# A two-layer memory-attention kernel with a planned instruction order: new plan figures, the V weights loaded in eight pieces, and a new order of tasks

## The chip, the cores and the metric

The kernel runs on one NeuronCore of a Trainium2 chip. A core has five engines that run side by side, each with its own in-order stream of instructions: TensorE (matmuls; PE in the profile, its weight loads PEld), VectorE (DVE), ScalarE (ACT), GpSimd (POOL) and SyncE (SP), which here only issues DMAs. Engines meet through semaphores. Matmul results go to PSUM, of which the kernel uses eight banks (`bank`), and are copied from there to SBUF by ACT or DVE. The metric is the device time of one execution in microseconds (us); less is better.

## The reference

The program is two identical layers over a sequence of 2048 rows of width 512; a layer is attention with a small recurrent memory, then a gated feed-forward block (FFN), each behind a layer norm and with a residual:

```python
for s in range(n_seg):                       # 64 segments of 32 rows
    xs = x[:, s*seg_len:(s+1)*seg_len, :]
    h = jnp.concatenate([mem, xs], axis=1)   # 8 memory rows + 32 rows
    q, k, v = h @ Wq, h @ Wk, h @ Wv         # 32 heads of 128
    p = _softmax(masked(q @ k.T * scale)); o = (p @ v) @ Wo
    mem = o[:, :M, :]                        # feeds the next segment
    outs.append(o[:, M:, :])
...
x = x + _A_ref(_layernorm(x), mem0, ...)     # attention
x = x + _B_ref(_layernorm(x), ...)           # (sigmoid(x@w_gate) * (x@w_up)) @ w_down
x = x + _A_ref(_layernorm(x), mem0, ...)     # second layer, same weights
x = x + _B_ref(_layernorm(x), ...)
```

(The einsums are abridged to products.) Inputs and output are bf16. Because `mem` goes from one segment to the next, a layer has 64 steps in a row that can't overlap.

## The kernel before

**Tiling.** Work is cut into 70 steps. In step t, `emit_step` treats segment t of layer 1 and segment t-6 of layer 2 together, so that a matmul has 80 moving columns (two times 8 memory and 32 sequence rows) while both layers run, and 40 in the first six steps and the last six, where one layer runs alone. A step makes q and k per head (L834, weights `wq_sb`, `wk_sb`), copies them (`qku`), scores (L848), softmax on DVE and ACT (L862 to L879), transposes the probabilities (L891), multiplies with V (L914, V rows in `vsb`) and projects with `wo_sb` (L932). The next step's q and k need the memory rows that come out of this L932. After every fourth step a block of 128 rows goes through `ffn` (transposes L1002, gate and up L1034, down L1058), whose weights POOL loads anew for every block.

**V.** V of the sequence rows doesn't depend on the memory. `v_pass` (L682) multiplies 128 normed rows with eight column groups of `wv_sb`, four matmuls of 512 columns for each, and writes the results through small staging tiles (slices of the FFN weights' tiles `wd`, `wg`, `wu` in the start-up) to a DRAM scratch `scr`. In the start-up eight such passes are made for layer 1 (`trace`, `v_group`). V of the memory rows is made within each step (`strips`, L759, 32 matmuls), staged in `sst` and sent to `vsb`. Steps read their V rows back from `scr` by DMA (L803).

**Start-up.** x blocks and all weights are loaded by SP (`load_x` L721, `pre1` L736, `load_weights` L583). A block is normed by `layernorm_T`: statistics on DVE (L638 to L640), a power on POOL (L641), scaling on DVE (L642), four transposes on PE (L651), then copies to `xvf` (the left operand of a V pass) or to `hT` (the input of a step). POOL first clears `qku`, `ptsb`, `pb` and `hT` tiles (`clear`).

**What sets the order.** Every piece of work is a task with a list of engines, a duration, a latency and keys for its dependencies (`Planner.add`). `plan` takes the tasks' priorities from the compressed table `SEQUENCE`. `forward` then plays the tasks through: each engine, when free, takes the ready task of highest priority whose buffers are free. It models DMA transfers as one bus: a transfer starts at least LEAD after its issue, takes bytes/BUS, and is taken as landed TAIL after its end, or at the issue's end plus `lat`, whichever is later. The instructions are then written out in the order of the planned starts, so a plan fixes the order on every engine but not the times. Where the plan leaves PE idle for over 0.25 us, `warm` (L410) puts matmuls on a zero tile `hot` (L1150) ahead of the next task, to keep its clock up. PE works in order, so they take their time whether the wait is there or not. For the large POOL transfers a manual dependency on a PE instruction (`pace`) keeps them from starting early. SP has at most eight transfers under way.

Of the kernel before, what the change touches and what calls it, by code (L numbers as in the profile page):

```python
# [17 lines left out]
AX = mybir.AxisListType  # L18
PSUM = bass.MemoryType.PSUM

P = 128
MEM = 8
SEG = 32
L = MEM + SEG
# [29 lines left out]
;AiJ8T3rAL|Nji^h>nE-)}}C6?#2*O0$8G4ZZdL%K2&sSfSGsr9F5bywiEpw1$9etJ{dj{n8$!UX!b>*%CVi0odWLR>PmMTURN8S`<`QSiresNn(7<<XH_|&hysZ(_+9io+E1yoPuJDs<%HrJ9~e&G  # L54
lO{?#YvSIBvP$R_;9f!1|GAlKk>X8^RhDlpmDnr7kt;6IZnSwn6|>@F3yW-VRO=#$!{s!|Z#sU*>kMf3XXFEnvc7`kKHK|1UA0@05#wb7a7HOlD?Yn#`J@z-(MeZ4Km`1|dy`f+^gMz@=%!FceG>$<
t$84$Kv|p6^^$~XKEw?)j1MY5bdV%#WrWw}B23to{C{XpW!a@PnfSMtcvtJ+x*0jL#Q{bGuEI}JeR4GK!d54vj>OKEncRQml~*<K;u1oaaQ4{bP`bof8*k|Jnvq^F=+Qyw{#`8!eH2|2^ft1nJbm7!
Ab!74vPh6M&l&LAlQ$kp(4RycR@9_lQx%SxC@=;7(#|M{pc-Zvq5^7mctV2pd4al%PqA<vseo$aQ(1$2O&p$$2=)#zF^2|o-u9XqFI-1Mc~jNaoYzdPrv`*zAA!u}T!KRNn7qKAo7WedWKFqAM5iWz
(lO=AI5ErprhTd6f)YVPYmhmHt`^X*krIWOe)K$vkW0fBn6t30v3~xgu9D9|2u?9Qhqxd3g!4-fxZSJdG?KXHi3=~m?P`o5>72)lIpD#^L81>xGR3Ji9|#WNB5L4{0_zR8rRp9-LS`%KDA3>to0^K8
trO%5X$z>-v_0tee?vxx^C`edFc{4p18&9J_1{77`WnlnpP=acza2)_2A~h&p}raH3Y3dS29jhXA=bf9kS8`f0IGrq5@}V)qI^z5??#c29baAb0B$86Cw+{B(m#uPRQTV>59ecM?f~YLiHK_agbl@M
>kXP60ej5O8Z1}7VtH~Tyi}o8Nh6os$k>dRMu$0U)mEux#MGAgPf!AyIq?@8yns1dXj`J(kB*bI#3S~kQG5MPNqKzX18+^sdBXNu6=5{T5Go1Hxs9?O$^vCQ9bSAntpCOL*N`Zy6d6f)8l}XGG}z!f  # L60
@(X9T<!k{a%zpTXjJr(t*vp+7A*WM2OF6JX&M0cCIFbCkn57sI8Q<FmQlDF2|3#N}6qtsBH%lb612z6V*1A9Y_A@HY$+fn$;9u1be-2ErQ~GLxg$2@V7S)+jTIXY3FAmgWqS`b0OT4UpsnQ7R$Uf33
f3q+HJ7f{+pc=}GM~NHQMP)4Ah>|J)wLO*-th<rKO_jdm{nOnoiY#EQdRE4_v%h|2_Nh`rzYRf!MHM6J(w85<_tb^)uriQo7uah{!`vFKpVnQ&1p}V2`ifjs&YA$@K)-I1;sCslWe)kvpEr4NIv$>b
$&(@1<pp8s;j>8S|K3v8wlu5u{sJg=#Rx9i+kw<LbAmj-UaSLL1MiR`VRCa!)$b@Ty6%s&&v4>}u`fQZ;+bdW<Ob3l-pr$_EMZQim=hbKvZ5di1HcO5lfzu>|J(t#K!!VbaFFOoH`q3<{|fuFn_mY>
N#qBHUB~tJpDBZzsN#V-j^HA?Zmp^VMr$l&wigZ!6G+n#Wl6+GCYi0!N}4?hlP<aS#+>w}!5feTN8x0LhVLxzf#j{MokfCkc2tntWi%)%a0+_sm}gKS<%9o?Qc^s3X%0c;+3$S4Zf`X_SMflE&zf_o
wPdTR?W}usM(6@KRBnkbX&xW`@27TFHa+~x-n1p7oNpmCO5t~VLj%|2TqGdh-$%(pp$yz?g00A>HskB6GJ(jKjZ%-2KC^<6@57J>vVrNoqFBsW(8oFdrnld-^_;3!9^BItXakbPlLz4Os~=#Z-UE;R
!5pJ^>pPsd&xhDnEIfA;NtUB2{lc`PNhDMNNNXgUt;Y_V(-IRN%Wwc@PoyIz-ja>r86o>5O#|&@Q_TB8>^5aEi+Hfh*7*WY89q>TGH}y*sZdAq>dlKh{IpyunqlyBE6}`&jeD%QD-bv-@nHELd#&I}
jU>HA@Gs*vv~NJiDWi6~+2-+z=+tAp_2U-kk;Oboz6}CNL=y1tO~SZt|5342>sk+++3Zo%f=GV#H&LgjhVM#tIBp=kP6Cgamu(<{{@8FLGHqAvecHiZs<xJ+H#)9rRR4+)jCexU3mvz-mae3hp`2-3
FEPSk2imif>V(3Sl-{H8mU_cf@*xkxDWOnFwz6c!FJAS;LFerNh?aQ%r4=4mH~gLO<$z5b@w4Q@enjX0N~+4I<4bOV<L&QMs{AL~K^68#PBIoXZyYl}7@JBOHk)VpuZay4Mxx^*F7O_4xh24*esQ8o
nJiw4^WFJh!Er-dsLy>K;Nq6yn&qnrwfILB6Ku+Yf&34Qc{UMk`|s*i&*91|h-!IU*TlOI872}YkcIyQYU32w)fOBYHh7v29KW1*UzoOY?kUUI&AMe8gG+bo(Rr{Qy8UIk&{FyxdC->kW!Idi6@8uR
;Yn>=xdDyJPyu4a9-gP~O4R2`^H@-jJf~NgrO%aCsaKOP2@eiTN7^rw3S>Wbb6m7kSk&+$2QO2>z6~d$B|g&kSQ*G4XuZCIrWn%6z&%`X@*9yt%q!`_ig+H}9RUtnAPLxlIczn_Gc%sk$h*ud5=Ya*  # L70
E#TQTKMYUuH2pWDS@=F{f9&PY_1gn%%>V7%1x0GNPa_w<H&lm72r#6MGH3LrUgY|O8=(u_?Q+wJS~O4cerm_Av#Z2y8Tb17OhXF8uz1Ht3k3MJ85>le-CmjBwlyVeo}tG|u?PusV|K{J<!sV?l76ZC
%ok0t)F8`NxWZia7Lj}pQgjV3bO&b*#gar0CKrt~3BPVv)Vc~=+8iqsz&GOhRv{yU0!If&f}=zT7Rloks0+0n;WS4drhidZ!f6XQyo`#U?bClZ@Dy!MUAD0hDv=3naO5w1GD<qB*(a|By8?O?gmhz<
F@Z7VI3sOOjwuE;n~M-gxqA<{L9H#%Lqka1?kjbvp=89ydelGO$}hiNwB=)#{NB&<8sTHg(yhvI2&bKR*=XH8@YK|96fX!s-3kf{;IAkc1j9?HUju>Zfkr^UXoHZkmz!Gf$;xu&+mVOIQ3|QGf6ZOy
Dkx$DU`6y#LGYZS#XgJbwLkowu$5?eQk=BCGYWt?q&H*)+YLHa53A);_H|Du<6t$5-sGTup)YLO1oot!TJR0iI9DO3+pH(TbIiX#L}71)Bp{_!1n-P%ErTQ}%8pG``{MTE`jUbQuon54^`Hu(RWB0P
klS-rS`0NyyY$W{?=R=8q`dqV<v6u;ntyFPA+C1IVTuOo_hYHhUPTz`VwmKi(o$>7>~qN<&ToL1A9!aNYl6b+ypgKcNis7?LeU*i<N-PVs$MYtrQ#naMkiB<N&4IDJ~%k_!`jlV4O9A8pWo+6e&Etf
RW)umy-K7u?Afx}$|cZH512hsVeog)JK&WS@wY<y&$8Y(JcWg%eEPQB)MOG1zmq$sZ6K|d4XJe#Y+r?TqTI*djB1{`D)$Q7Ytlv1AO%K)vXzD;)b}>7KvA~@O<5zyg?!?9T6}4M|4{wIpjPrZ0?j>M
@gv1n_n9|s;dy^fMo<jXM(as<6BL*Srxp>rm&4@*^xU5+llyIJ{~dMh?E`D~elC54%Zg(E^#ZWDD!G}UBVkMSLh0g;2US!Tn66DSu!z#QEQ(<ZA1OXgzHh0*iMg#xqTW0<=XJCfBOR!gd*6OFo<fU;
*<%9I{zm~grt_(TXqn{hgb+gJ0L0vyTy}|E`^2N*?z=mtf=m4C;o?jl_<O>`tbdW2);*XL1xOS;&Kw6*cT?zv$z1K$&_qbYyq>gHj<GS}a3JfD)am1Oe84}~Po4TP90m@#A1Pm3!l9Rf0G^y|em8w`
0rk?#KOKi?&`|f&+0(At6FZ<t_GS^sd*q&X;1e>>6=jRXedTw_zbHdn2t#5}rCeIP@uX3;-scABupggrqaZ`}9UV=B9u`1xGjJWm02J%L{&f95iMdRkWz#zG=-W#3+&7Z5{`ZF=5KV0LU^Oabhbz)B
Y1lTm(kfI^u7L#XF5lf!g_GcSyXGPAV#J3buSt=VQ<@U&_U9%cx0EAw`qy9H&!zJl_~t%Qx<N=xC0TcH=Hk)j^{fCKF7VZX@S?}jE;&zz7M&xbz!UQiD6&>nXM%}%?Xu}gD=O*!0j_6hg}eNe*&A(+  # L80
hsIHMJA8Nny7zcUzP+D!LOLqUHCcjx<x{<=u}f@G5z(I?xMX{YJo^vLjEbpfnH*5ue&&`};ZM#IRGf3}^2S%<UXk%t#&QS+RH?$mzO^)<lsuhPABB{&@CI^9JV2~K%5KLE!-E!o?f+RK6#Y<;2@Wl0
!6Sz*tlq`48-^^bcv^S(?UufRbe64U01iI$b6csPrOM+Ysq)+z&SH8!E1B^uw}t3&@oJa$<PEAhp4{b`2t7Iq{ZEB{FUSWH6nA9p3;0JI*v^3fa!lOvwQQh@m9zpFfQBJB9OT8y6-ufR^eCGDRXn-j
W479R>{rDHRbOQJp|RTD-hZ>gI1oQc^7TKIDN%oZhPR~q^4!xuAOw0P%3TlI3p!6n+jImwNz00+u;^mh(O{bx8L}{YF)fL1T*XHTkg8@2Rzr<Vw_j1ON%E;WH3`uw*3eJi6G1d;aG6tJZB0EfF6~jW
Wq0N<tEz2$iUs=uZV`b)KBAKy<8xEtF1uQl47v*%!@7>o^8W~Lm51dA{?pv6-wtbc?)KzyY<0?)Uq({iTN$`ni=|vw5>R>_(2-(ws&?+ezL5#PPfmD|%it@}#V6PP^YVkXOFbLrB=Fl?)d&xPQZ{LQ
>HmznolcMn8qQ~kEV*a6?l9kAc|iU&RdBW@8fIdr2#P!*{(lmQ{?4{jr!iWgyXpW`+!ipG354+9gj6q~baBf~P#%92N<yTsRN;Z}qU-83x?K#gz<J@`nw`P6C|WS4qrc1JuZc5{Zq{$iLnm0O6PloB
{a~42^GsmQB^>ulcifoh&TZ;tpH$2cy>~8?3eJKQFtFxojwm-+Q0xNrc_A?0pGJh1Jb!re_Md^Lw(8LUX?bKW1@hHS0!H<F9KjWv?=iaYy{e?^5Q)sc`sOk*A+UM!GvkTsU<Ay&fk(UiM-E$ZL7-<T
WR-!@omdRJu*B3a8UzECk$+L9pZs9(DzQbQeFmgsiI!Cd$LDRLaOcOO!Imsy{CR1CNsw2W_YO*~uqS2x0F|0H$FfdJG`xpEtM4j2nvTJyZ(@|aH3>S{?v=|jRbU9*(tIJOQ!QP?b2!>=sT~ey#M{g|
Ni`HC)Y!?O^bIA%4sJCA<(IQ!o$;0^y+n?U5IrSb+=oiICBtPsXe`_`yMAhS?`*V%*2Q-3fJs5Klr;N|!$~GBMNlnROz(}POr(ois0P4WF1p1~2~Axh@Dlr2zRyHe!G1gT4TP2edUwq+sdxj<hdfp;
6_38TbNQ#9(1w}@PUKnDFqvhC<pXN1Imn#6s{igJZY-hx`vyFgV3%=$K9}&@`hD~UfX0%(Xz?Ru!ez$I){HUr&tU5C7OmTkTaYivEc~G$0~Xi+OW@e~_B~4QHj$e-2|Flg?pYi_?k=1m1P)=ZZoFm#
L1+REWb}1eqF)rqa9rOU##hTLKyWmER4yMNXR4WqomuM`8oM$w7yYlyNI^Wm*IEm!RsKgnX1gI{ky?92()eLB@KBvu6t}YRn{`8cW4FzK>$|JXr$j;+7QOW!e@x<ms5wdDMcHYJEXt1U6oCq>pM_(#  # L90
Q69~+ibL`c!31h7r8WEx`XYvvRenMpSc86gBOu(W(q19v{>Z}K7->?t4-r6TD(Bg>r%cCi=Cn-karKT7J*n@Q9keU@OR$6Bx`4e6I&5%~>h}p)l>B<}Q;*y2P-E-<_E&v??9RY2OlUWIkY8zP`PUnL
SWIce0!u#)?h2qFA4@M~TRit(cEJ6(1%|JePjWiE6d3M?nyGh0Tt_S0&FAb&%mM=C?|%;=kwLwn@V6+L8<y5JfER7=FmwaliagfMxN5Vm2Md#aL9uz&#m6CI8)HdODaRG(FzNd~t3dG3HV8%oMv<-O
SC1^^xJGhM$9%<_klNJ6SoP*>iq#-X2&j$*5-RgxaVz+h_t}HgOob=j{&z#iK;GX&iP~VtO6bEg@rv0&K(Eo9dB65=Pm%=8DVD;epB|M%4sqez@#{TCB(?h2AY{|5UQu_FLfj)hgbP1N1F#SFn>*VK
X455aqMK$LX6e$>p1sR*rg1aKX1MPh)+d%irA4cb30-Nr3HkSfc!gF1{&ocA$u+5RjFi%sVzFVwe?g#&kspwl$>q8P%0%@K1heWrrp?~}Lr&PSbR~2`HV9aaEYw2eC8o!2Zi0m9|1$ZB-k8)>xG!HB
2Xi(}O%u`87t*=&;^|RcIBfOnxAUv!W}4N?_GID9V=Ut#YPv|WrDWoSRk$4P#q>SjPwhRfACRwTxcFY)qi%AIXdun)+WS!gTa|TBFG*a4Z%$kNSnx7kMWbz7D0C0%XaioV#*|r=0=LPr`gkUcP-PQd
U<6GHD%|p=qq<w=8wigQ*@@6xUiX%Xlz9gL2?nr=+jho78djz_1Y*v4J=U@XVEehMNC*}GQS<B678b+MVhj+-U3hg^WaDRN7;xBu1ReY07DZWh)nXj)MReJ#o+SSRkRZw;Sk6U__St1fq6t&rq@84B
)3NwvVJl&5ou@J1Jxiw(h1fsReWqmUo#-0oP+RWC%cAz`rUb<tdk2{{9*ovAJnx<LQz5X*Kk|PqU$|>>K$fnxyLI*=0f<`ZjX+}Jx)d=E6aVLLqm}da+GwozMp(6_XUL%|<zH|5?pAoL+u+CYTQ`I!
^BWx)J~dn>k9!~B^z^@U21VKfuL-pDgGfH-8X)30`ex@Bisbx2VhJ%l23s9O+d}SWmPq|Q^~7lc*Or+SDDZtl=V6|vm?RQD?j6E1YASB72H1zE3;ld{wCuSt?T__nGWF~JEn9^))`)IJ?sUt(5$;t!
# [55 lines left out]
class Task:  # L154
    __slots__ = ("eng", "dur", "lat", "fn", "deps", "succ", "tail", "boost", "ndep", "ready", "start", "idx", "on", "fresh", "acq", "rel", "durs", "tick", "prev", "land", "adj", "banks", "rate", "nb")

    def __init__(self, eng, dur, lat, fn, boost):
# [6 lines left out]
        self.adj = {}  # L164
        self.banks = ()
        self.rate = 0.95
        self.nb = 0


class Buf:  # L170
# [18 lines left out]
class Planner:  # L189
# [79 lines left out]
    def forward(self):  # L269
        T = self.tasks  # L270
# [6 lines left out]
        bus = 0.0  # L277
# [944 lines left out]
```

## Time and profile before

| | |
|---|---|
| time, three runs | 1808.74, 1810.51, 1812.94 us; median 1810.51 |
| profiled execution | 1809.62 us |
| its span, first to last instruction | 1807.9 us |
| PE busy | 1781.7 us, 99% of the span |
| filler matmuls (L1150) | 97, busy 25.4 us |
| DVE, ACT, POOL busy | 1152.3, 1189.6, 580.5 us |
| granted TensorE clock | 1.00 |

The span is the profiled execution's from first to last instruction; 1.7 us lie around it. PE's busy time counts the filler matmuls as well, so the time in which PE does none of the reference's work is its idle time and theirs together. A matmul's own duration holds its passage through the array; matmuls in a row overlap, so what one costs is read from the chain of waits, where groups of them have the time they add.

### The profile page before, as it was taken

How to read it: one execution, taken by the hardware profiler on the slowest of the kernel's cores; microseconds unless marked ns; L12 is line 12 of the kernel's file. 1: busy time of each engine (PE TensorE's matmuls, PEld its weight loads, DVE VectorE, ACT ScalarE, POOL GpSimd, SP SyncE). 2: the span in 40 equal slices, each digit the busy share in tenths (PEclk: the TensorE clock that was granted, in tenths of full speed). 3: DMA queues.
4: the chain of work that ended last, by engine and by line, in shares of the span. 5: the costliest groups of instructions: out<-in, count | busy, mean ns of one | idle time of the engine just before them, and what ended most of it. 6: DMA issues, size and time to landing. Idle time of an engine off the chain costs nothing.

```text
span 1807.9 us, 92108 instructions
## 1 busy us (share of the span) xinstructions
PE 1781.7 (99%) x40039; PEld 1524.2 (84%) x40039; DVE 1152.3 (64%) x3919; ACT 1189.6 (66%) x2987; POOL 580.5 (32%) x838
## 2 busy tenths in 40 slices
PE   8999999999999999999999999999999999999998
PEld 4588888988888888989898888988888888889886
DVE  4466665665566666665666667666666676566665
ACT  6666766676667666666766666666665666666664
POOL 6413032423233243323324241323334231333422
PEclk9999999999999999999999999999999999999999
DMA  9825254635455454545546463545546453554543
GB/s 345 277 66 151 58 151 117 196 109 156 136 160 153 129 171 143 144 125 160 160 132 194 128 183 89 167 138 162 155 142 180 122 143 114 157 154 133 170 123 109
DMA packets 136872, 271.19 MB, mean 150 GB/s; under 512 B 32650, under 2 KB 69138, under 8 KB 136466
## 3 DMA queue, kind: packets, MB, share of 16 engines
q0 software_dynamic: 56928, 184.07, 34.4%
q1 hardware_dynamic: 79538, 81.22, 15.6%
q8 instruction: 314, 5.14, 1.2%
q14 instruction: 92, 0.75, 0.1%
HBM read 220.93 MB, written 26.21 MB: 137 GB/s over the span
## 4 chain that ended last, share of the span: by engine, by line
PE 89%; DVE 4%; ACT 3%; DMA 1%; issue 1%; SPq 0%; POOL 0%; ACTq 0%; DVEq 0%; POOLq 0%
PE bank L834 31%; PE bank L932 16%; PE bank L1034 11%; PE bank L682 8%; PE bank L759 7%; PE bank L1058 5%; PE bank L914 4%; PE bank L848 4%; PE bank L891 2%; DVE st L862 1%; ACT ptsb L1158 1%; PE bank L651 1%; ACT qku L1158 1%; DVE small L867 1%; DVE small L874 1%
## 5 line engine op out<-in xcount | busy, mean ns | idle before, releaser
L834 PE MATMUL bank<-hT,wk_sb 128*128 128x80 bf16 (+1 forms) x8960 | 622.2, 198 | 0.8 <-issue 0.7
L834 PE MATMUL bank<-hT,wq_sb 128*128 128x80 bf16 (+1 forms) x8960 | 622.2, 198 | 0.1
L1158 ACT CAST qku<-bank 128x480 bf16<-128x480 f32 (+3 forms) x770 | 387.9, 513 | 220.8 <-PE bank L834 141.3
L834 PEld LDWEIGHTS <-wq_sb 128*128 128x128 bf16 x8960 | 455.2, 99 | 35.6 <-issue 22.2
L834 PEld LDWEIGHTS <-wk_sb 128*128 128x128 bf16 x8960 | 450.9, 99 | 0.6 <-issue 0.6
L862 DVE TENSOR_TENSOR st<-bank,cst 40x240 f32<-40x240 f32 (+3 forms) x768 | 278.3, 367 | 234.3 <-PE bank L848 227.0
L932 PE MATMUL bank<-otsb,wo_sb 128*128 128x80 bf16 (+1 forms) x8960 | 363.4, 198 | 5.4 <-ACT otsb L1158 4.4
L932 PEld LDWEIGHTS <-wo_sb 128*128 128x128 bf16 x8960 | 338.0, 99 | 21.3 <-issue 8.1
L1026 POOL DMA_DIRECT2D wg<-in_B_w_gate_dram x217 | 164.4, 758 | 268.1 <-PE bank L1034 107.6
L1027 POOL DMA_DIRECT2D wu<-in_B_w_up_dram x217 | 163.9, 755 | 259.0 <-PE bank L1034 110.6
L1052 POOL DMA_DIRECT2D wd<-in_B_w_down_dram x217 | 153.7, 708 | 251.6 <-PE bank L914 82.3
L1158 ACT CAST otsb<-bank 128x480 bf16<-128x480 f32 (+3 forms) x420 | 198.0, 483 | 54.2 <-PE bank L914 40.3
L1158 ACT COPY ptsb<-bank 40x240 bf16<-40x240 bf16 (+3 forms) x559 | 177.9, 320 | 46.1 <-PE bank L891 36.6
L872 ACT ACTIVATE st<-st 80x240 f32<-80x240 f32 (+3 forms) x420 | 158.5, 381 | 43.5 <-DVE st L869 40.0
L1034 PE MATMUL bank<-xnT,wg 128*128 128x128 bf16 (+2 forms) x1784 | 171.6, 218 | 0.2 <-ACT xnT L1158 0.2
L1034 PE MATMUL bank<-xnT,wu 128*128 128x128 bf16 (+2 forms) x1784 | 171.1, 218 | 0.0
L874 DVE TENSOR_REDUCE small<-st 80x6 f32<-80x240 f32 (+3 forms) x420 | 151.2, 362 | 29.5 <-ACT st L872 27.1
L641 POOL TENSOR_TENSOR small<-small,cst 128x1 f32<-128x1 f32 (+1 forms) x80 | 45.2, 566 | 379.1 <-DVE small L640 360.9
L848 PE MATMUL bank<-qku 128*128 128x80 bf16 (+1 forms) x2240 | 160.6, 198 | 1.8 <-ACT qku L1158 1.5
L869 DVE TENSOR_TENSOR st<-st,small 80x240 f32<-80x240 f32 (+3 forms) x420 | 154.1, 368 | 3.5
L879 DVE TENSOR_TENSOR pb<-st,small 80x240 bf16<-80x240 f32 (+3 forms) x420 | 153.5, 369 | 4.0
L867 DVE TENSOR_REDUCE small<-st 80x6 f32<-80x240 f32 (+3 forms) x420 | 151.7, 362 | 4.6
(95 smaller groups left out, 2327.7 us busy)
## 6 DMA issues: line engine op xcount, KB each, us to landing
wg<-in_B_w_gate_dram POOLq DMA_DIRECT2D x220, 256.0 KB, 4.4
wu<-in_B_w_up_dram POOLq DMA_DIRECT2D x220, 256.0 KB, 4.3
wd<-in_B_w_down_dram POOLq DMA_DIRECT2D x220, 256.0 KB, 4.3
vsb<-scr SPq DMA_DIRECT2D x476, 48.0 KB
vsb<-sst SPq DMA_DIRECT2D x480, 32.0 KB
scr<-vst SPq DMA_DIRECT2D x120, 96.0 KB
wk_sb<-in_A_Wk_dram SPq DMA_DIRECT2D x10, 384.0 KB
wq_sb<-in_A_Wq_dram SPq DMA_DIRECT2D x10, 384.0 KB
```

The costliest lines, as they stand in the source:

```text
L834: nc.tensor.matmul(o_ap, lhsT=W[:, c, h * P:(h + 1) * P], rhs=mv(c), start=(c == 0), stop=(c == DC - 1))
L848: nc.tensor.matmul(s_all(SB)[:, w0 + i, :], lhsT=fview(qku[:, i, 0, 0:1], [(1, P)]), rhs=qku[:, i, 1, 0:ncol], start=True, stop=True)
L862: pl.add("DVE", dve_ns(n, True), lambda gsz=gsz, hs=hs, st=st, SB=SB, pj_=pj_, npj_=npj_, mk=mk, idx=idx: nc.vector.tensor_tensor(out=st[p ...
L867: pl.add("DVE", dve_ns(n), lambda hs=hs, st=st, mx=mx: nc.vector.tensor_reduce(out=mx[pr, hs], in_=st[pr, hs], axis=AX.X, op=ALU.max), r=s ...
L869: pl.add("DVE", dve_ns(n), lambda gsz=gsz, hs=hs, st=st, mx=mx: nc.vector.tensor_tensor(out=st[pr, hs], in0=st[pr, hs], in1=mx[pr, hs].uns ...
L872: pl.add("ACT", act_ns(n), lambda hs=hs, st=st: nc.scalar.activation(out=st[pr, hs], in_=st[pr, hs], func=ACTF.Exp, scale=self.scale), r=s ...
L874: pl.add("DVE", dve_ns(n), lambda hs=hs, st=st, sm=sm: nc.vector.tensor_reduce(out=sm[pr, hs], in_=st[pr, hs], axis=AX.X, op=ALU.add), r=s ...
L932: nc.tensor.matmul(WB[:, c * ncol:(c + 1) * ncol], lhsT=self.wo[:, h, c * P:(c + 1) * P], rhs=otsb[:, hl, 0:ncol], start=(h == 0 and c == ...
L1026: pl.add("POOL", 760, lambda wg=wg, fs=fs: nc.gpsimd.dma_start(out=wg[:], in_=self.wgv[:, :, fs]), r=[("wo", self.H - 1)], w=[gk] + bt, la ...
L1027: pl.add("POOL", 760, lambda wu=wu, fs=fs: nc.gpsimd.dma_start(out=wu[:], in_=self.wuv[:, :, fs]), r=[("wo", self.H - 1)], w=[uk] + bt, la ...
L1034: nc.tensor.matmul(gu[:, 2 * i + k, 0:n], lhsT=W[:, c, i * P:(i + 1) * P], rhs=xnT[:, c, rw], start=(c == 0), stop=(c == DC - 1))
L1158: nc.scalar.copy(out=dst, in_=src)
```

## The change

Four things are edited; the functions are otherwise the same.

1. Figures of the plan: when each engine can start (FIRST), a slower bus in the first 18 us (BUS0), a shorter LEAD and TAIL, and shorter latencies of several transfers.
2. The V weights are loaded in eight pieces of four heads (512 KB) in place of two of four and three of eight. Each piece from the third on waits for the piece two before it, on SP.
3. The three clears of `vsb` may go to ACT alone (before: ACT or DVE).
4. A new `SEQUENCE`, from which a new order follows on all five engines, from start to end.

```diff
 SEQUENCE = r"""
...
-    BUS, LEAD, TAIL, BIG, ROOM, POOL0 = 345.0, 2000.0, 1900.0, 300000, 1.0, 2000.0
+    BUS, BUS0, SLOW, BIG, ROOM, TAIL = 345.0, 290.0, 18000.0, 300000, 1.0, 1200.0
+    LEAD = {"SP": 1000.0, "POOL": 1800.0}
+    FIRST = {"PE": 0.0, "ACT": 2040.0, "DVE": 980.0, "POOL": 3500.0, "SP": 750.0}
...
-        free = {"PE": 0.0, "ACT": 0.0, "DVE": 0.0, "POOL": self.POOL0, "SP": 0.0}
+        free = dict(self.FIRST)
...
-                    bus = max(bus, now + self.LEAD) + tk.nb / self.BUS
+                    bus = max(bus, now + self.LEAD[e])
+                    bus += tk.nb / (self.BUS0 if bus < self.SLOW else self.BUS)
...
-            pl.add(("ACT", "DVE"), {"ACT": 1760.0, "DVE": 2200.0}, ...   # vsb clears
+            pl.add("ACT", 1760, ...
...
-        for h0, n in ((0, 4), (4, 4), (8, 8), (16, 8), (24, 8)):
+        for h0, n in ((0, 4), (4, 4), (8, 4), (12, 4), (16, 4), (20, 4), (24, 4), (28, 4)):
             cs = slice(h0 * P, (h0 + n) * P)
-            ld(self.wv[:, :, cs], wv_v[:, :, cs], P * self.DC * n * P * 2, [("wv", h) for h in range(h0, h0 + n)])
+            tk = ld(..., [("wv", h0 - 8)] if h0 > 4 else [])
+            if h0 > 4:
+                tk.after = pl.writer[("wv", h0 - 8)]
...
+                if tk.after is not None:
+                    self.tc.add_manual_dep(nc.cur_bb.bb.instructions[-1], seen[tk.after], self.SYNC, reason="transfers one after another")
```

Latencies (`lat`, ns) that change: weights and start-up x 4000 or 2500 to 1750 (L583, L721, L736); `scr` to `vsb` 5000 to 4300 (L803); `sst` to `vsb` 3500 to 3200 (L814); FFN weights 5200 to 4700 (L981, L1026, L1027, L1052).

What the new order does on the engines, as the two programs' instruction lists show it:

- PE has the same matmuls but for the fillers, 89 in place of 97. Ahead of the first V matmul stand 44 fillers of 21,376 columns in place of 25 of 12,032; behind it 45 of 18,432 in place of 72 of 30,464.
- In the start-up SP asks for x blocks 3, 1, one of those held in `hff`, 7 and 0 in this order, in place of 1, 0, ... DVE norms blocks 1, 3, 7 and 0, one after the other, before PE comes to the first V pass, which needs blocks 0 and 1 alone; before it normed 1 and 0 first.
- POOL does the first power after six clears in place of thirteen. The `vsb` clear that DVE did is on ACT.
- The first q and k of step 0 come after 11 V groups in place of 24 and a strip. The last V group of the start-up stands late in step 1; before, it stood at the end of step 0.
- From step 2 on, no stage gains or loses work; tasks change places with their neighbours.

## The prediction

> **What bounds the kernel now.** I read the page's head and granted clock first, then the chain of waits, then PE's own waits, then tables by stage.
>
> ```profile
> PE 1781.7 (99%) x40039; PEld 1524.2 (84%) x40039; DVE 1152.3 (64%) x3919; ACT 1189.6 (66%) x2987; POOL 580.5 (32%) x838
> PE 89%; DVE 4%; ACT 3%; DMA 1%; issue 1%; SPq 0%; POOL 0%; ACTq 0%; DVEq 0%; POOLq 0%
> ```
>
> PE does nearly everything that sets the end, and its work is the same after the change. So only the time in which PE does no such work counts: 1807.9 - 1781.7 = 26.2 us idle, and 25.4 us of fillers (L1150). The tables of busy time by stage say where. Idle is a stage's length less its PE time: these lines are of all PE work,
>
> ```profile
> 0.00:11.88 11.88, 7.52 (x38) 3.07 (x38) 7.14 (x21) 6.63 (x11) 9.20 (x32) 1.00 0.83 260
> 11.88:80.00 68.12, 66.91 (x606) 34.97 (x607) 23.88 (x74) 45.36 (x91) 33.91 (x63) 1.00 1.01 342
> 80.00:106.00 26.00, 24.43 (x718) 20.58 (x717) 17.62 (x67) 15.72 (x53) 6.93 (x11) 1.00 0.35 101
> 280.00:1690.00 1410.00, 1400.92 (x31444) 1229.55 (x31441) 919.15 (x3115) 939.50 (x2304) 458.35 (x634) 1.00 0.51 148
> ```
>
> and these of the fillers alone (first column PE, then its weight loads):
>
> ```profile
> 0.00:11.88 11.88, 7.04 (x25) 2.53 (x25) 1.00 0.83 260
> 80.00:106.00 26.00, 3.58 (x15) 1.19 (x15) 1.00 0.35 101
> 106.00:141.50 35.50, 5.15 (x21) 1.58 (x21) 1.00 0.26 72
> 141.50:280.00 138.50, 2.29 (x9) 0.67 (x9) 1.00 0.41 118
> 1690.00:1792.10 102.10, 5.00 (x18) 1.31 (x19) 1.00 0.46 132
> 1792.10:1804.60 12.50, 2.38 (x10) 0.56 (x8) 1.00 0.32 95
> ```
>
> In 280 to 1690 us PE is idle for 9.1 us in 1410: no order can win much there. The start costs 11.9 us before the first V matmul; from there to 80 us PE has 1.2 us idle and no filler. Then come 1.6 idle + 3.6 fillers at 80 to 106, 1.0 + 5.2 to 141.5, and near the end 2.9 + 5.0 and 0.1 + 2.4. The fillers' busy time holds overlap with neighbours, so a stage's loss lies between their bare columns (0.21 us for 512) and that figure.
>
> The timeline shows what sets the start:
>
> ```profile
> 1.00 4.17 PE L1150 MATMUL bank<-hot 128*128 128x512 bf16 x13 [1.00 <-DVE cst L557]
> 7.34 0.57 POOL L641 TENSOR_TENSOR small<-small,cst 128x1 f32<-128x1 f32 x1
> 7.95 0.99 DVE L642 TENSOR_SCALAR xn<-xs,small 128x512 bf16<-128x512 bf16 x1 [2.06 <-POOL small L641]
> 9.23 1.89 PE L1150 MATMUL bank<-hot 128*128 128x512 bf16 x8
> 11.88 1.04 PE L682 MATMUL bank<-wv_sb,xvf 128*128 128x512 bf16 x4 [0.15 <-ACT xvf L1158]
> ```
>
> The first block's statistics are done at 4.05, but POOL is clearing tiles until 7.34; its power releases the scaling, the transposes, and with a second block the first V pass.
>
> **What the Trainium skill says.** "TensorE: Matmul & The Clock Gate", section "Wait — 56ns, not 53.3ns?", gives a 512-column matmul 215.7 ns start to start when warm and 426.7 cold. The trace agrees: 12 V matmuls add 2.60 us in the chain (217 ns each); the first 13 fillers take 4.17 us, between both. "Perfetto Trace Analysis", "Identifying the Most-Contended Engine", warns that matmul busy time is no distance to the roofline; so I count removable waits and fillers, not the 1%. "Advanced Engine Details and Errata", "VectorE Performance Modes", says that VectorE's second SBUF port is shared with GpSimd: the first scaling, beside POOL's clears, took 0.99 us, the next ones 0.41. "DMA: Bandwidth & Descriptors", "Issuing engines are not separate DMA queues": all DMAs share the same engines. The trace agrees in that its DMA share is 1.01 at 342 GB/s through 11.88 to 80 us.
>
> **The start, step by step.** Block 1's x is now the second DMA without weights ahead of it. The first was issued at 0.75 and used at 2.95; 0.45 us later that is 3.4. Statistics 0.69 + 0.18 + 0.15 give 4.5. POOL has six clears instead of thirteen, from 3.09: five at 0.44 and one of 0.23, so 5.5; power 0.57, 6.1; scaling beside clears 0.99, 7.1. PE transposes block 1 at 7.1 (before: block 1 at 9.0). But then DVE, in order, norms block 3 (its statistics stand behind that scaling: 7.1 + 1.0 = 8.2; POOL is through its clears at 8.6; power and scaling, 9.6 to 10.2), then 7 and 0 together (2 x 0.69 + 4 small ones of 0.15 to 0.18 = 2.0, so 12.0; block 0 is the 2.1st MB that SP asks for, and before, 3.15 MB had landed at 14.06 and 0.79 MB at 4.95, so some 10.4, in time). Power, power, scaling add 0.57 + 0.57 + 0.41: block 0 is scaled at 13.5. PE meanwhile does fillers: 13 after block 1's transposes (2.8 us), 11.25 after block 3's (2.4), 1 and 3.25 later; from 7.1, with four sets of transposes at 0.22, they alone fill PE until 13.9. Transposes of block 0 then, 3.25 fillers (0.7), and two `hT` copies and one `xvf` copy on ACT (0.26 + 0.21 + 0.44): the first V matmul at about 15.0, between 14.3 and 15.8. **Loss 3.1 us** (2.4 to 3.9). The earlier power wins nothing, because block 0 comes fourth.
>
> **V weights in eight pieces.** 4.2 MB as before. SP's wait for the piece two before it holds every DMA behind it (x, `wq`, `wk`), but at that place the same eight-transfer limit waits anyway: before, SP waited for `wv` 1.8 us at most. V group k needs piece k; pieces 3 and 4 stand at 2.9 and 3.5 MB, landed by 13.3 and 15.1 us at the rate above, used at 16.8 and 17.6; pieces 5 and 6 at 5.2 and 5.8 MB, 19.5 and 21, used after 21. Cost 0, the cover being the V groups at 0.87 us; without it each late piece would cost 1 to 2 us. The second left operand waits for a DVE and an ACT copy, some 0.6 us idle; before, block 14 and the wait for its x, at 29.6, cost 0.9. For 15 to 80 us I take 1.5 us idle against 1.2: **loss 0.3** (-0.5 to 2).
>
> **The `vsb` clear on ACT.** Three at 1.89 us from 2.04 end at 7.7; ACT's first other work waits for transposes at 7.3. Cost 0; if transposes came sooner, 0.4.
>
> **The steps behind it.** Step 0's q and k come 13 V groups sooner, 11 us of other work, so its chain of softmax is underway while V groups remain, and the last of these lie in step 1. Step 1's end had 15 fillers of 2.55 us bare columns (5.2 us lost with idle); now one of 0.64. **Gain 3.6** (2.2 to 4.3): 5.2 less 0.7 and some 0.9 idle. Steps 2 and 3: bare fillers 3.6 to 3.0, **gain 0.6**. To 280 us: 1.5 to 1.1, **0.4**. 1690 to 1792: 3.2 to 2.8, **0.4**. Their idle time I leave as it was.
>
> **The end.** Of 1.8 us bare fillers between the last step's L932 and the end 0.2 remain; one L1034 group goes ahead of the transposes L1002. But the chain L932, `oxT` copy, transposes, norm, L1034 takes 4.3 us from 1792.1 whatever fills it, so only the work moved ahead counts: **gain 1.0** (0 to 1.8).
>
> **The middle.** The order changes, but per step the work between the last L932 and the next q and k is on average 1.8 us against 1.9. Shorter latencies let PE come up to 0.7 us sooner to transferred weights; FFN weights land in 4.4 us, and the new plan still allows 0.76 + 4.7. So 0 ± 1.5.
>
> **Sum.** 3.1 + 0.3 - 3.6 - 0.6 - 0.4 - 0.4 - 1.0 = -2.6 us. The profiled execution of 1809.6 (span 1807.9, 1.7 around it) becomes 1807.0; the runs' median lies 0.9 above it, so **1807.9**. A measurement here tells about 0.2%, 3.6 us, from no change.
>
> **Rivals.**
>
> *Late weights (slower).* By the instruction lists, at the durations of the chain, q and k of heads 7 to 32 now come in one run at 67 to 72 us, before in pieces from 44 to 79. The last `wk` piece stands at 17.6 MB of SP's transfers, before at 18.8 (issued at 69.7). With POOL's fewer V writes it should be issued 5 us sooner and land at 67, 4 us ahead of need. SP also carries 1.2 MB of V writes up to there, before 0.5, and each waits on an ACT copy. From 4 us late on, PE waits for every further us, `wo` too: at 10 us late, +6, so 1814. For it: the DMA share of 1.01. Against: PE never waited for weights before. Chance 0.17, 1811 to 1822.
>
> *The start is not repaid.* Step 1's softmax chain still waits on DVE and ACT with V groups beside it, since their copies (0.58 us each) share ACT. Only half of the 3.6 comes, nothing at the end: 1810.7 (to 1814). For it: ACT waits in the chain at 80.5. Chance 0.15.
>
> *More is won.* The fillers' whole busy time counts and the middle wins 1.5: 1804 (1801 to 1806.9). Chance 0.17.
>
> *It does nothing.* Excluded as such: instruction lists differ everywhere; a wash is inside the forecast's range.
>
> **Chances.** Forecast 0.51, own range 1804.5 to 1811.5; about a third of it lies below 1806.9. Faster: 0.17 + 0.17 = 0.34. Slower (above 1814.1): 0.12 of late weights and 0.04 from the others, 0.17 with rounding. Same: 0.49. The range 1803 to 1814 leaves out the far end of both tails.
>
> **What would show it.** First L682 matmul at about 15.0; no DMA among PE's waits; fillers at 80 to 106 us at most 1 us; PE idle plus fillers after 106 us some 2.4 us less. The forecast is wrong if PE waits for `wk_sb` or `wo_sb` at 65 to 85 us, if V starts after 16 or before 14, or if the middle's idle time moves by over 2 us.

## The result, and the profile after

The changed kernel takes 1805.6 us (median of 4 runs, 1805.1 to 1807.0) where the kernel before took 1810.2 beside it: 0.9974 of the time, 95% interval 0.9957 to 0.9991. A second comparison, with 16 runs, gave 1806.7 us and 0.9980 (0.9972 to 0.9987). So it is some 4 us faster: both intervals lie below 1, with upper ends of 1.6 and 2.4 us less. The forecast was 1807.9.

Lines of the file lie 8 further down from L624 on (L642 is L650, L682 is L690, L1150 is L1158). The page of the changed kernel, busy time and the chain by engine:

```profile
PE 1767.0 (98%) x39806; PEld 1523.7 (84%) x40031; DVE 1162.7 (64%) x3926; ACT 1185.7 (66%) x2980; POOL 573.6 (32%) x828
PE 86%; DVE 6%; ACT 4%; issue 2%; DMA 1%; SPq 1%; POOL 1%; POOLq 0%; ACTq 0%; DVEq 0%
```

Of PE's matmuls 39,806 were recorded against 40,031 weight loads (before 40,039 of each). So PE's busy and idle time can't be set against each other between the two kernels; the weight loads, one for each matmul, are complete, and distances below are counted on them, from the start of one to the start of the next. The stages answering to those of before, all PE work, then the fillers alone:

```profile
0.00:15.76 15.76, 11.60 (x61) 5.34 (x61) 8.85 (x23) 8.78 (x14) 9.19 (x33) 1.00 0.91 291
15.76:80.00 64.24, 63.11 (x628) 34.13 (x639) 25.95 (x82) 42.43 (x85) 27.03 (x50) 1.00 1.01 331
80.00:106.00 26.00, 25.55 (x725) 20.95 (x730) 15.00 (x56) 18.10 (x55) 4.66 (x8) 1.00 0.34 99
280.00:1690.00 1410.00, 1390.86 (x31248) 1229.87 (x31434) 926.51 (x3126) 935.65 (x2297) 458.19 (x634) 1.00 0.52 148
```

```profile
0.00:15.76 15.76, 11.19 (x44) 4.44 (x44) 1.00 0.91 291
80.00:106.00 26.00, 0.81 (x3) 0.22 (x3) 1.00 0.34 99
106.00:141.50 35.50, 4.67 (x18) 1.34 (x18) 1.00 0.26 76
141.50:280.00 138.50, 1.75 (x7) 0.49 (x7) 1.00 0.44 123
1690.00:1786.64 96.64, 4.28 (x16) 1.09 (x16) 1.00 0.47 135
1786.64:1800.00 13.36, 0.33 (x1) 0.10 (x1) 1.00 0.36 105
```

The 15 fillers at 80 to 106 us have become 3, the 10 of the last stage 1. The start in the timeline:

```profile
5.21 0.57 POOL L649 TENSOR_TENSOR small<-small,cst 128x1 f32<-128x1 f32 x1 [0.74 <-DVE small L648]
5.82 2.49 DVE L650 TENSOR_SCALAR xn<-xs,small 128x512 bf16<-128x512 bf16 x1 [0.69 <-POOL small L649]
7.42 0.74 POOL L570 MEMSET hT<- 128x160 bf16 x4
8.60 2.97 PE L1158 MATMUL bank<-hot 128*128 128x512 bf16 x13
15.76 2.12 PE L690 MATMUL bank<-wv_sb,xvf 128*128 128x512 bf16 x8 [0.17 <-ACT xvf L1166]
```

The power is 2.1 us sooner than before, the scaling behind it takes 2.49 us in place of 0.99 and ends just after a row of POOL's clears, and V starts at 15.76.

To compare stages, a step of the recurrence is taken as ended where the 128th and last weight load of its output projection (L932) begins. All profiles (us; "lands" is when DVE begins the first statistics):

| kernel | x lands | first V | step 0 | step 8 | step 63 | step 69 | PE's end |
|---|---|---|---|---|---|---|---|
| before | 2.95 | 11.88 | 85.83 | 255.63 | 1671.85 | 1791.92 | 1804.53 |
| changed | 4.03 | 15.76 | 83.40 | 253.44 | 1670.77 | 1786.64 | 1799.80 |
| after_again2 | 3.40 | 15.12 | 83.32 | 254.07 | 1671.39 | 1787.34 | 1800.49 |
| rest_before | 4.78 | 18.20 | 89.39 | 259.41 | 1677.68 | 1797.48 | 1810.09 |
| end_before | 3.56 | 15.29 | 83.44 | 253.26 | 1670.49 | 1789.76 | 1802.38 |
| middle_before | 3.38 | 15.12 | 83.94 | 254.55 | 1671.07 | 1787.04 | 1800.37 |
| start_before | 2.99 | 13.58 | 86.56 | 256.77 | 1676.06 | 1792.25 | 1805.59 |
| clears_later2 | 3.46 | 16.57 | 84.17 | 254.60 | 1672.32 | 1789.30 | 1802.46 |
| unpaced2 | 3.40 | 16.81 | 85.51 | 256.65 | 1674.15 | 1789.91 | 1803.07 |
| no_end_fill2 | 2.96 | 11.88 | 85.01 | 255.66 | 1672.39 | 1791.64 | 1804.11 |
| clears_act | 3.33 | 13.71 | 81.91 | 251.62 | 1669.24 | 1784.82 | 1797.97 |
| clears_act_wo | 4.76 | 14.44 | 83.46 | 254.43 | 1671.21 | 1787.26 | 1800.41 |
| best | 3.46 | 14.24 | 82.38 | 252.49 | 1669.14 | 1785.24 | 1798.58 |
| end_order | 2.91 | 13.22 | 86.19 | 256.33 | 1673.11 | 1790.93 | 1805.44 |

For the changed kernel against before: 2.2 us won up to step 8, 1.1 lost from step 8 to step 63 (1417.33 in place of 1416.21), 3.7 won from there to the end. In the second profile of it (after_again2): 1.6, 1.1 and 3.6.

Four of these profiles (rest_before, start_before, unpaced2, end_order) show a granted clock of 0.86 between 8 and 20 us, the others 1.00. There V begins 1.3 us or more late, so their starts are not set against the others'.

### The profile page after: what moved, and what is told of

It is laid out like the page before. It is cut to its first block, busy times and chain, and to the rows that moved or that the text cites. A ratio compares the mean times of both kernels' runs of the same rounds, so it can differ in the third digit from the quotient of the medians.

```text
span 1803.3 us, 91862 instructions
## 1 busy us (share of the span) xinstructions
PE 1767.0 (98%) x39806; PEld 1523.7 (84%) x40031; DVE 1162.7 (64%) x3926; ACT 1185.7 (66%) x2980; POOL 573.6 (32%) x828
## 3 DMA queue, kind: packets, MB, share of 16 engines
q8 instruction: 314, 5.14, 1.2%
## 4 chain that ended last, share of the span: by engine, by line
PE 86%; DVE 6%; ACT 4%; issue 2%; DMA 1%; SPq 1%; POOL 1%; POOLq 0%; ACTq 0%; DVEq 0%
PE bank L842 30%; PE bank L940 15%; PE bank L1042 10%; PE bank L690 8%; PE bank L767 7%; PE bank L922 4%; PE bank L856 4%; PE bank L1066 3%; PE bank L899 2%; ACT ptsb L1166 1%; DVE st L870 1%; DMA vsb<-sst 1%; PE bank L659 1%; DVE small L882 1%; DVE pb L887 1%
## 5 line engine op out<-in xcount | busy, mean ns | idle before, releaser
L842 PE MATMUL bank<-hT,wq_sb 128*128 128x80 bf16 (+1 forms) x8960 | 621.7, 198 | 0.7
L842 PE MATMUL bank<-hT,wk_sb 128*128 128x80 bf16 (+1 forms) x8960 | 621.3, 198 | 0.0
L842 PEld LDWEIGHTS <-wq_sb 128*128 128x128 bf16 x8960 | 454.2, 99 | 35.5 <-issue 24.4
L842 PEld LDWEIGHTS <-wk_sb 128*128 128x128 bf16 x8960 | 450.5, 99 | 0.0
L1034 POOL DMA_DIRECT2D wg<-in_B_w_gate_dram x217 | 163.8, 755 | 272.6 <-PE bank L1042 159.3
```

Of the source, the lines that this page charges most:

```text
L842: nc.tensor.matmul(o_ap, lhsT=W[:, c, h * P:(h + 1) * P], rhs=mv(c), start=(c == 0), stop=(c == DC - 1))
L1034: pl.add("POOL", 760, lambda wg=wg, fs=fs: nc.gpsimd.dma_start(out=wg[:], in_=self.wgv[:, :, fs]), r=[("wo", self.H - 1)], w=[gk] + bt, la ...
```

## The experiments

### Parts of the two orders put together

`SEQUENCE` is a ranking of all tasks, so a kernel can rank its tasks by one kernel up to a point of the plan and by the other behind it, with that kernel's planning figures for those tasks:

```diff
+    OTHER = ((1803, 13303),)                  # ranks that are the other kernel's
+    OTHER_LAT = {4300.0: 5000.0, 3200.0: 3500.0, 4700.0: 5200.0}
...
+            if any(a <= k < b for a, b in self.OTHER):
+                T[i].other = True
+                T[i].lat = self.OTHER_LAT.get(T[i].lat, T[i].lat) if T[i].eng != ("PE",) else T[i].lat
...
-                    bus = max(bus, now + self.LEAD[e])
+                    bus = max(bus, now + (2000.0 if tk.other else self.LEAD[e]))
```

**rest_before.** 

> The changed kernel up to about 250 us of its plan (step 8); from there on the order and the planner's figures of the kernel before. Theory A (the difference is made in three places that add up: steps 0 to 8 of the recurrence end 2.2 us earlier in the changed kernel, steps 9 to 40 give about 2 us of it back, the end wins some 4 us): this kernel keeps the 2.2 us of the start and has the middle and the end of the kernel before, so 2.2 us less than before (1.5 to 3), and its step 40 ends 2 us earlier than before's. Rival B (a different order moves the time by 2 us or so anywhere, by accidents of the buffers, and nothing adds up): anything from 4 us less to 2 us more, with step 40 where the changed kernel has it.

Measured: 1809.4 us against 1810.9 of before beside it, ratio 1.0000 (0.9991 to 1.0008), so no gain is shown. The medians differ by 1.5 us, but the interval ends at 1.6 us less and leaves A's 2.2 out. Its profiled execution is its longest of 13 (1815.7), and lost its time in the start, in code that is the changed kernel's. The row of 8 to 20 us (the 0.86 is the granted clock), and the fillers there:

```profile
8.00:20.00 12.00, 10.65 (x54) 5.00 (x56) 8.23 (x24) 2.79 (x11) 4.43 (x12) 0.86 1.10 345
```

```profile
9.36 4.66 PE L1158 MATMUL bank<-hot 128*128 128x512 bf16 x13
```

The same 13 fillers took 2.97 us where the clock was 1.00. So this run doesn't confirm A's share of the start; that rests on the profiles and on start_before. It shows what the low clock costs in the start: step 0 ends at 89.4, 6 us behind the changed kernel.

**end_before.** 

> The changed kernel up to 1645 us of its plan (step 63); from there on the order and the figures of the kernel before. Theory A: the end's gain is gone and the rest is as in the changed kernel: 0 to 1.5 us less than before, and some 3.5 us more than the changed kernel; fillers at the end about as many as before had (27). Rival C (the end's gain is not the order of the end but a phase that the stages ahead hand on): this kernel ends within 1 us of the changed one.

Measured: 1809.5 us, 0.9995 (0.9986 to 1.0003). From step 63 on it needs 131.9 us, as before (132.7), where the changed kernel needs 129.0; up to there it is the changed kernel. A holds; C, an end within 1 us of the changed kernel's, falls.

**middle_before.** 

> The changed kernel up to step 8 and from step 64 on; between them the order and the figures of the kernel before. Theory A: it avoids the 2 us that the changed kernel loses between steps 8 and 40, so it is 2 us faster than the changed kernel and some 6 us faster than before. Rival D (the 2 us are lost because the changed start hands the middle another phase): the same time as the changed kernel within 0.7 us. Rival B: no better than the changed kernel, and possibly worse.

Measured: 1806.1 us, 0.9977 (0.9968 to 0.9986): no better than the changed kernel by the times. That is what D and B said. By its profile step 8 to 63 takes 1416.5 us (changed: 1417.3), so 0.8 is avoided there, not 2: my reading up to step 40 had left out that 1.2 us of it come back by step 63. That is too small for these times to show. In the table five profiles with the old middle take 1416.2 to 1416.8 us, and seven with the new one 1416.8 to 1417.7; the sixth and eighth, rest_before and start_before, take 1418.3 and 1419.3, so what comes before the middle can cost it more than its order does.

**start_before.** 

> The kernel before up to about 101 us of its plan (the end of step 1: five V pieces, V begins at about 11.9 us), from there on the order and the figures of the changed kernel. Theory A (what PE waits at the start is paid back at 80 to 106 us, since the same V matmuls then fill gaps that before left open): the early V start is worth little, and the time is 0 to 2 us above the changed kernel, with fillers and waits at 80 to 106 us as in before (about 3.6 us). Rival E (the 3.9 us by which V starts later are lost for good, and the gain at 80 to 106 us is due to the order there): 2 to 4 us below the changed kernel.

Measured: 0.9993 (0.9987 to 1.0000), so 2 us or more above the changed kernel: E falls, and A's upper edge is passed. The old start is no asset: at full clock, in the profile of before, step 0 ends 2.4 us behind the changed kernel, with V begun 3.9 us ahead of it. The profile of this run is one with the low clock; it loses 3.3 us to the changed kernel up to step 8 and 2.0 more up to step 63, with the same ranking and figures there. So the parts don't simply add up, as B said in part.

### The start

**after_again2.** 

> The changed kernel itself, beside the other three on one chip. Expected: 0.9974 of before again (0.9960 to 0.9990), some 4.6 us less, with the first V matmul 11.73 us after the first x lands, as in the three profiles that have this start.

Measured: 1806.7 us, 0.9980 (0.9972 to 0.9987), V 11.72 us after the first x: as expected.

**unpaced2**, V pieces without their wait:

```diff
-            tk = ld(..., [("wv", h0 - 8)] if h0 > 4 else [])
-            if h0 > 4:
-                tk.after = pl.writer[("wv", h0 - 8)]
+            tk = ld(...)
```

> The changed kernel with its eight V pieces, but without the rule that two are under way: neither the dependency in the plan nor the wait on SP; the order of all engines is the same. Prediction's step (the pieces cost nothing): the same time within 0.7 us. Rival H (SP's waits for the earlier pieces at 5 to 14 us hold back the x loads queued behind them and with them the normalisations and the first V matmul): SP's issues up to 14 us come 1 to 3 us earlier, and with them the first V matmul by up to 1 us; or, the other way, the pieces crowd out the x rows that the first normalisations need, and the V start comes 1 us or more later.

Measured: 1806.5 us, 0.9979 (0.9972 to 0.9986), the same as after_again2, and SP issues no sooner: its fourth V piece is issued at 7.93 us, the changed kernel's at 7.68 and 8.38 in its two profiles. So the wait costs nothing that these times show: without it SP stands at the same place anyway. H falls. (Its profile begins V at 16.81, with the low clock, as in rest_before.)

**clears_later2**, the clears moved behind the fourth power:

```diff
+        late = [tk for tk in order if tk.on == "POOL" and tk.idx < 17 and tk.start > 6000.0]
+        order = [tk for tk in order if tk not in late]
+        at = max(k for k, tk in enumerate(order) if tk.on == "POOL" and tk.dur == 575 and tk.start < 13000.0) + 1
+        order[at:at] = late
```

> The changed kernel with the eleven GpSimd clears that ran beside the first scaling put behind the fourth power on POOL; the plan and every other engine's order are the same. Expected of the scaling itself: 0.41 to 0.5 us in place of 2.49, and the first V matmul some 2.0 us earlier (about 9.7 us after the first x lands). Theory F (step 0 is held at about 74 us by the last wk piece, which comes at the pace of a DMA stream that is full from the start on, so the start is repaid by waiting): the 2 us turn into a wait of the projection matmuls at 72 to 74 us, and the time is that of the changed kernel within 0.7 us. Rival G (PE is the bound from the first V matmul on): step 0 ends 2 us earlier and the time is 1.5 to 2 us below the changed kernel.

Measured: 1808.9 us, 0.9990 (0.9983 to 0.9996), slower than after_again2 by 2.2 us by the medians; neither F nor G said so. The first scaling took 0.41 us, as expected. But the clears now ran beside the fourth scaling, block 0's, on which V waits. The timeline, POOL and DVE:

```profile
12.31 0.50 POOL L574 MEMSET ptsb<- 128x480 bf16 x1
14.68 0.42 POOL L572 MEMSET pb<- 80x384 bf16 x1
12.40 2.84 DVE L650 TENSOR_SCALAR xn<-xs,small 128x512 bf16<-128x512 bf16 x1
```

It ended at 15.24, 0.14 us after the last clear (15.10), as the changed kernel's first scaling ended at 8.31, 0.15 after its last (8.16). The first scaling of before shows the same (0.99 us, ending 0.14 after this last clear of its row):

```profile
8.23 0.57 POOL L564 MEMSET hT<- 128x160 bf16 x3
```

So does the changed kernel's second (0.47 us, 0.15 after a single clear). With the clears the slow scaling moved, from the first to the fourth, and where POOL has none of them (clears_act, below) none is slow. So the clears cause it, and a scaling that meets a row of them waits for the whole row. The Trainium skill ("Advanced Engine Details and Errata", "VectorE Performance Modes") says that GpSimd instructions and VectorE's two-port ones block each other. The runs agree, and show the size: up to 2.4 us on an operation of 0.41. V began at 16.57, 1.45 us later than in after_again2. The 2 us that I expected had the cause right and forgot the fourth scaling.

**clears_act**, the same eleven clears written by ACT, in its idle time at 9 to 13 us and between later copies:

```diff
+        late = [tk for tk in order if tk.on == "POOL" and tk.idx < 17 and tk.start > 6000.0]
...
+        act = [k for k, tk in enumerate(order) if tk.on == "ACT" and tk.start > 9000.0]
+        for tk in late:
+            tk.on, tk.fn = "ACT", self.zero[tk.idx]      # copies of a zero tile
...
```

> The changed kernel with the eleven clears that ran beside the first scaling written by ACT instead (seven in its idle time at 9 to 13 us, four later between its copies); plan and all other orders the same. Expected: no scaling over 0.5 us, the fourth one done at about 12.8 us (its x lands at about 10.2), the first V matmul at 14.0 to 14.3 us, 1 us before that of the changed kernel. Theory F (the last wk piece of the full DMA stream decides when step 0 ends): that 1 us comes back as a longer wait of the projection matmuls at 72 to 75 us (1 to 2 us in place of 0 to 1.1), step 0 ends at 83.3 to 83.9 as in the changed kernel, and the time is the same within 0.6 us. Rival G (PE bound from the first V matmul): step 0 ends at 82.3, 1 us less in all.

Measured: 1805.2 us, 0.9971 (0.9960 to 0.9982), the lowest median here.

```profile
5.12 0.41 DVE L654 TENSOR_SCALAR xn<-xs,small 128x512 bf16<-128x512 bf16 x1 [0.70 <-POOL small L653]
13.71 2.55 PE L694 MATMUL bank<-wv_sb,xvf 128*128 128x512 bf16 x11 [0.16 <-ACT xvf L1179]
```

V begins at 13.7 and step 0 ends at 81.91, both 1.4 us sooner than in after_again2; PE shows no wait at 72 to 75 us. So here the earlier start is kept, against Theory F; by the times the gain over after_again2 isn't told from nothing. F came from waits like this one of middle_before (PE's waits: total, times, longest; and the weight load that waits):

```profile
PE bank L842 <- issue: 1.1, 1, 1.1
```

```profile
73.82 0.17 PEld L842 LDWEIGHTS <-wk_sb 128*128 128x128 bf16 x4 [1.19 <-issue]
```

The changed kernel's own start had 0, 0.4, 0.4 and 1.1 us of it in four profiles, 0.9 and 2.2 in the two with the low clock; before had none. It is not a wait for a weight transfer: in the program neither this weight load nor the matmul ahead of it waits for a semaphore, and the last q and k loads that do wait for a transfer, 23 to 31 loads earlier, passed without a wait in middle_before. It goes with another DMA queue of the page (packets, MB, share of 16 engines):

```profile
q8 instruction: 314, 5.14, 1.2%
```

The program has 80,360 instructions for PE, and 64 bytes for each are these 5.14 MB; the page's other such queue, q14, has 0.75 MB, which is 64 bytes for each of the other engines' 11,700. So the packets of q8, 256 instructions each, are by their size PE's own program on its way to PE. In all ten profiles with the changed start the weight load at this place begins 1.36 to 1.60 us after a packet of q8 has ended, whether it had to wait (in middle_before the packet ended at 72.46 and the load before this one began at 72.54) or not (clears_act: 70.33, and 71.68). So PE most likely stands there for its next instructions. No edit tested that, and why the packet is late in some executions is not shown.

**clears_act_wo**, in addition three `wo` pieces put behind the last `wk` piece:

```diff
+        wo = [tk for tk in order if tk.idx in (75, 76, 82)]
+        order = [tk for tk in order if tk not in wo]
+        at = next(k for k, tk in enumerate(order) if tk.idx == 80) + 1
+        order[at:at] = wo
```

> As the one with the clears on ACT, and three wo pieces of 0.39 MB (first used after 79 us) that SP issues at 26 to 47 us are put behind the last wk piece, so that this piece comes some 3 us earlier. Theory F: no wait of the projection matmuls at 72 to 75 us is left, step 0 ends about 1 us earlier than in the changed kernel (82.2 to 82.8), and the time is 0.7 to 1.3 us less. If the moved wo pieces come too late, L940 waits for them at 79 to 83 us instead. Rival G: no difference to the kernel with the clears alone.

Measured: 1805.9 us, 0.9973 (0.9961 to 0.9984), not told apart from clears_act. SP issued the piece at 57.7 us in place of 60.1, and yet the same weight load waited 0.9 us from 72.4 on (its packet of q8 ended at 71.97). So it is not that piece, which fits the account above, and F falls in its cause.

**best.** 

> The start of the changed kernel with both of these edits, the order and figures of the kernel before between steps 8 and 64, the changed order and figures from there on. If the three parts add up: the changed kernel's time less 1 us (start) and less 0.8 us (the middle, where the two profiles of the changed order took 1417.3 us from step 8 to step 63 and the order of before 1416.2 and 1416.5): 1804.3 to 1805.3 us, about 0.9970 of before. If the parts don't add up: as the changed kernel, 0.9975 to 0.9980.

Measured: 1806.1 us, 0.9972 (0.9961 to 0.9983), between the two expectations. In the profile step 8 to 63 takes 1416.65 us, 1.0 less than in clears_act (1417.63), and PE ends 1.9 us sooner than in after_again2; the times don't separate it from the changed kernel or from clears_act. By the profiles clears_act and best beat both kernels; by the times they beat before alone.

### The end

**no_end_fill2**, the kernel before without its end's fillers:

```diff
-            if gap > 250.0 and on:
+            if gap > 250.0 and on and tk.start < 1675000.0:
```

> The kernel before without its filler matmuls after 1675 us of the plan (27 instructions, some 7.4 us of PE time as the profile counts it). Theory I (the fillers stand only in waits that are there anyway, and the end's gain of the changed kernel is its order): the same time as before within 0.7 us. Rival K (the fillers run past the waits and delay the work behind them): 1 to 3 us less than before, which would be a good part of the changed kernel's gain at the end. Rival L (without them PE's clock is granted less in the last steps): slower than before, with a clock under 1.00 after 1700 us.

Measured: 1810.6 us, 1.0000 (0.9991 to 1.0008): Theory I. The fillers stand for the most part in waits that are there anyway. L falls: the granted clock stays at 1.00 without them. K's lower edge, 1 us less, isn't excluded by the interval, and the profile comes near it. The stage tables, steps 64 to 69 and what follows, of before,

```profile
1671.85:1791.92 120.07, 117.22 (x3291) 99.04 (x3288) 80.17 (x280) 75.10 (x239) 41.56 (x58) 1.00 0.49 142
1791.92:1804.60 12.68, 12.61 (x206) 7.95 (x202) 5.02 (x17) 3.08 (x12) 3.21 (x5) 1.00 0.32 94
```

of no_end_fill2, steps 64 to 69 (0.8 us shorter),

```profile
1672.39:1791.64 119.25, 113.41 (x3264) 98.16 (x3271) 80.12 (x280) 75.07 (x239) 41.57 (x58) 1.00 0.50 143
```

and of the changed kernel:

```profile
1670.77:1786.64 115.87, 113.67 (x3260) 97.90 (x3268) 79.24 (x273) 75.17 (x244) 41.24 (x57) 1.00 0.50 145
1786.64:1799.90 13.26, 11.98 (x216) 8.24 (x211) 5.59 (x19) 3.15 (x12) 3.46 (x5) 1.00 0.36 106
```

Steps 64 to 69 are 4.2 us shorter, and what follows up to PE's last matmul 0.5 longer (13.15 for 12.62). Summing in the trace the distance from each weight load to the next, by line of before, shows where the 4.2 are:

| steps 64 to 69 | before | changed |
|---|---|---|
| L932 x768 | 22.61 | 21.62 |
| L891 x96 | 4.45 | 3.96 |
| L834 x1536 | 40.38 | 39.91 |
| L914 x96 | 7.34 | 6.92 |
| L759 x224 | 13.20 | 12.88 |
| L848 x192 | 6.10 | 5.96 |
| fillers x17, x16 | 2.97 | 2.70 |
| L1034 x288, x272 | 15.36 | 14.39 |
| L1058 x40, x38 | 5.92 | 5.78 |

The last two are work put off: 16 L1034 and 2 L1058 now stand behind the last step, where before had nine more fillers. At 0.056 and 0.216 us in the chain they are 1.3 us. The rest, some 3 us, is the same matmuls with less waiting among them. It lies in few, long waits. Count a weight load as waiting where its distance exceeds its line's median (0.025 to 0.056 us), leaving out fillers and, for their uneven distances, L759 and L1058: by over 0.25 us this happens 15 times in before, 5.9 us in all, and 7 times in the changed kernel, 2.7 us (2.5 in after_again2). The shorter excesses hold 6.5 and 6.8 us. Every kernel here with the old end has 13 to 18 long ones (5.3 to 8.4 us), every one with the new order and figures 5 to 8 (1.9 to 3.5). What ends them is not shown: for most the profile names no releaser.

**end_order.** 

> The kernel before, with the changed order of tasks from step 64 on, but planned there with its own old figures (transfer times of 3.5 and 5.2 us and so on). The plan then places the same tasks elsewhere. Theory M (the end's 3.6 us are won by an order that fits the new figures; the order alone is not enough): less than 1.5 us won against before. Rival N (the order of the tasks alone wins it): 3 to 4 us less than before.

Measured: 1810.9 us, 1.0001 (0.9993 to 1.0009): Theory M. Steps 64 to 69 take 117.8 us, half of the gain (1.3 us of it work put off, as in the changed kernel, and 9 long waits of 4.2 us), but 14.5 in place of 12.6 follow. So the ranking alone is worth nothing; together with the figures it was made for it is worth 3.6 us. The new figures with the old ranking were not tried.

## Why the prediction was right or wrong

**The start: size right, one step wrong, others covering it.** V was to begin at 15.0, between 14.3 and 15.8; it began at 15.76 and 15.12. "Scaling beside clears 0.99" was the step that failed: it took 2.49. That figure was taken over from before, where four clears stood behind the power, to a kernel where ten do; before's own trace had the scaling end with the last of them. That the start came out in its range all the same is luck: the power came at 5.21 and not at 5.5, at 4.6 or so in the profiles where x lands at 3.4, since POOL began its clears 1 us sooner than in the profile before (2.04 for 3.09), and from block 1's transposes to block 0's PE was filled for 6.1 us, not 6.8. The fillers as PE's limit held: with the first x given, V follows 11.7 us later in four profiles at clock 1.00.

**Eight pieces at no cost, second operand's 0.6 us idle.** Right as far as it was tested: unpaced2 shows that the wait between pieces costs nothing, and the changed kernel's profile has no wait of PE for `wv_sb`; eight pieces against five were not compared alone. The one longer wait of L690 in the start was 0.6 us.

**15 to 80 us, "loss 0.3": wrong way.** Set against PE's work done up to there (every matmul counted at its line's median distance), the changed kernel is 3.55 us behind where V begins and 1.90 behind at step 0's end, so it won 1.6 us in between; in the second profile 1.1 (2.91 and 1.83). Nothing here shows by what.

**Step 1's end gains 3.6.** Right: on the same count it is 1.23 us ahead at step 1's end, so this step won 3.1 us, in the second profile (1.29 ahead) also 3.1. The steps to 280 us, for which I took 1.0 together, gave up to step 8 1.0 in the first profile and 0.3 in the second. So the stages to step 8 win 2.2 and 1.6 where the steps of the sum give 1.2 (3.6 + 0.6 + 0.4 - 3.1 - 0.3).

**The middle, 0 ± 1.5.** It lost 1.1, inside. By the distances of weight loads it is no long wait (excesses over 0.25 us: 50.6 us in before, 50.2 and 49.8 in the changed kernel) but short ones: behind the transposes L891 2.3 us are lost, behind q and k (L834) 2.0 won, and smaller sums elsewhere; nothing here shows more.

**The end: the term that was mis-sized.** "1690 to 1792: 3.2 to 2.8, 0.4. Their idle time I leave as it was" is the step that failed. Without the 1.3 us put off, steps 64 to 69 won 2.9. I had counted bare fillers and held the rest constant; but most of the waiting stands between matmuls of one line, where the plan put no filler, and what was won are the long waits there, from 5.9 to 2.7 us. "The end", gain 1.0, came out as 0.8 (1.3 of work in 0.5 us). Together 3.6 in place of 1.4.

So the sum was -2.6 and is -4.7 in the first profile, -4.0 in the second: 1.0 and 0.4 more at the start, 1.1 less in the middle, 2.2 more at the end. Measured 1805.6 and 1806.7 lie in the range, the first nearer to the 1804 of the rival "more is won", the second to the 1807.9 forecast; and what was won more is not what that rival named, since the middle lost. "Late weights" was not seen: the waits at L842, 0 to 1.1 us in profiles at clock 1.00, aren't for weights. "Start not repaid" fell.

## What to carry to other kernels

When an order is replanned, count the waits among the matmuls that stay, and the long ones apart, not only the fillers: sum the distances from one weight load to the next, by line and stage, in both traces. Where a planner's order wins, take rank and figures as one thing; the rank alone did not give the end's gain. Where an engine waits and the profile names no releaser, see whether the program has a semaphore there before a transfer is blamed. And keep rows of GpSimd clears away from a VectorE scaling that starts a chain: put them on ACT where it idles, and look which scaling they meet next.

## What the hardware showed unexpectedly

- A scaling of 128 x 512 bf16 on DVE took 0.41 us alone and 2.49 or 2.84 us beside ten or eleven GpSimd memsets in a row, ending 0.14 to 0.15 us after the last of them. Statistics of the same size took 0.67 to 0.69 us beside them or not, and ACT's zero copies beside a scaling cost it nothing (0.40 to 0.41 in clears_act).
- In two of ten profiles that begin with the changed start's fillers the granted clock was 0.86 between 8 and 20 us, and V began 13.4 us after the first x in place of 11.7. The old start isn't spared: two of its four profiles had the same, with V at 13.58 and 13.22 in place of 11.88. What decides it is not shown.
- One weight load of step 0 began 1.36 to 1.60 us after a packet of the instruction queue q8 ended, in ten of ten profiles with the changed start, and PE stood still for it for 0 to 2.3 us.
- The middle can repeat almost exactly: step 8 to 63 took 1417.33 and 1417.32 us in two profiles of the changed kernel. In other kernels with the same ranking there it took 1416.8 to 1419.3.
